# Where the row maxima of an attention step are kept: SBUF tile or spare columns of the PSUM tile

## The chip, the cores and the metric

The kernel runs on one core of one Trainium2 chip. The metric is the device time of one execution in microseconds, the median of several runs. A core has five engines that work through their own instruction queues and wait for each other by semaphores: TensorE (PE in the profile; PEld is its weight load), VectorE (DVE), ScalarE (ACT), GpSimd (POOL) and SyncE (SP, which here only issues transfers). TensorE writes its results to PSUM; VectorE and ScalarE reach both PSUM and the large on-chip memory SBUF; GpSimd works on SBUF alone in this kernel.

## The reference

Two layers in a row, for 8 batch entries of 576 tokens.

```
scores = 0.125 * q @ k^T                        # 8 x 8 heads, 576 x 576, head size 64
thresh = max(scores, last axis) - tau           # tau = 0.02
scores = where(scores >= thresh, scores, -1e9)
attn   = exp(scores - max(scores));  attn /= sum(attn) + 1e-9
x      = attn @ v                               # heads side by side: 576 x 512
h      = relu(x @ w_in);  u, v = halves of h    # 512 each
v_n    = (v - mean) / sqrt(var + 1e-6)          # over the 512 columns
v_s    = w_spatial @ v_n + b_spatial            # mixes the 576 tokens
out    = (u * v_s) @ w_out
```

The first four lines matter here. Per row of scores a maximum is needed before the exponentials, and only scores within tau of it count.

## The kernel before, in words

The attention is cut into 144 steps, 18 for each batch entry. A step `g` takes 128 query rows of a pair of heads and all 576 keys of both, and runs through these functions:

- `scores` and `scores_end` (L685, L696, both through `part`, L672): 16 matrix products on TensorE (L678) write the scores of both heads into one of two PSUM tiles, `s_ring[g % 2]`. Such a tile is `[128, 1536]` fp32 (L130)[...]. The scores of head 0 lie from column 96 to 671, those of head 1 from column 864 to 1439 (`at = (96, 864)`, L658). The columns from 672 to 863 hold nothing.
- `top` (L702, called by the token `M`): one VectorE reduction (L705) reads both heads' scores from PSUM and writes the two negated row maxima into a small SBUF tile `negm`, `[128, 2]` fp32, taken from the pool `small`.
- Then a step goes one of two ways, fixed by the lists `ON_ACT` (L84) and asked by `on_act(g)` (L660). 83 of the 144 steps are thresholded on ScalarE, 61 on VectorE.
  - On ScalarE: `shift` (L708, token `B`) is one VectorE `tensor_scalar` (L711) that turns `negm` into (scale times) minus maximum plus tau, in place in SBUF. `spread` (L714, tokens `E` and `F`, one for each head) has ScalarE compute Prelu of score plus that bias with a slope of 1e30 below zero (L719), so that all scores under the threshold become hugely negative. `exps` (L737, token `Z`) takes the exponential of it all (L739).
  - On VectorE: no shift. `spread` takes exp of score minus maximum (L722), and `mask` (L731, token `W`) zeroes on VectorE what lies under exp(-tau) (L734).

So for a step on ScalarE the order is: reduction L705, shift L711, two activations L719, one activation L739; the shift can be asked for at once behind the reduction or some instructions later. The two PSUM tiles alternate, so the matrix products of step `g + 2` must wait until the activations of step `g` have read its scores.

The probabilities are then transposed by transfers (or by TensorE for some), multiplied with v (`pv`, L376 and L381, divided on VectorE at L388 and L390), and the second layer's matrix products (L529, L576, L605, L634) with their evictions are woven in between the steps. GpSimd rearranges and converts loaded data (L192, L215, L341) and does the normalization of v (`moe_v`: L545, L557 to L561); all of this goes from SBUF to SBUF.

The order of all of it on each engine is written out by hand: the strings in `ORDER` (L16) list tokens such as `M5:0` or `B5:0`, and `run_token` (L884) issues them one after the other under a manual schedule (L940). Neither a planner nor priorities move them. The four strings serve batch entries 0, 1, 2 and all later ones, so that from the third entry on the iterations are nearly alike. Tokens for the way that a step does not take are skipped (L897).

Of the kernel before, what the change touches and what calls it, by code (L numbers as in the profile page):

```python
# [8 lines left out]
F32 = mybir.dt.float32  # L9
# [78 lines left out]
def kernel(  # L88
# [17 lines left out]
    nc = tc.nc  # L106
    B, H, S, D = q.shape
    assert (B, H, S, D) == (8, 8, 576, 64)
    scale = 0.125
# [3 lines left out]
    P = 128  # L113
# [4 lines left out]
    small = ctx.enter_context(tc.tile_pool(name="small", bufs=6))  # L118
# [11 lines left out]
    s_ring = [ps_s.tile([P, 1536], F32, name=f"s{i}") for i in range(2)]  # L130
# [50 lines left out]
    def view(t, off, dims):  # L181

        return bass.AP(t.tensor, t.offset + off, [t.ap[0]] + dims)
# [476 lines left out]
    def on_act(g):  # L660

        return g % 18 in ON_ACT[min(g // 18, len(ON_ACT) - 1)]
# [37 lines left out]
    negm = {}  # L700

    def top(g):  # L702

        nm = negm[g] = small.tile([P, 2], F32, name="negm")
        nc.vector.tensor_reduce(out=nm, in_=view(s_ring[g % 2], at[0], [[at[1] - at[0], 2], [1, S]]), axis=AX.X,  # L705
                                op=ALU.max, negate=True)

    def shift(g):  # L708

        nm = negm[g]  # L710
        nc.vector.tensor_scalar(out=nm, in0=nm, scalar1=scale if steps[g][1] == 4 else 1.0,  # L711
                                scalar2=float(tau), op0=ALU.mult, op1=ALU.add)

    def spread(g, h):  # L714
# [146 lines left out]
    steps = []  # L861
# [22 lines left out]
    def run_token(tok, it):  # L884
# [15 lines left out]
        m = 2 * b + a[0] if a else 0  # L900
        if kind in "SGYMEFBZW":
            {"S": scores, "G": turn_bank, "Y": scores_end, "M": top, "E": lambda g: spread(g, 0),
             "F": lambda g: spread(g, 1), "B": shift, "Z": exps, "W": mask}[kind](g)
        elif kind in ("QA", "QB", "qa", "qb"):
            task("q", i, kind[1] in "Bb")[1 + (kind[0] == "q")]()
# [135 lines left out]
```

## Time and profile before

Time: 450.61 us, median of 3 runs (450.59 to 450.75). Span of the profiled execution: 448.5 us; the granted clock of TensorE was 0.996.

| engine | busy us | share of the span | instructions |
|---|---|---|---|
| TensorE products | 416.1 | 93% | 5035 |
| VectorE | 400.8 | 89% | 615 |
| ScalarE | 388.6 | 87% | 649 |
| GpSimd | 176.9 | 39% | 403 |

| operation | count | busy us | mean ns |
|---|---|---|---|
| L705 reduction, VectorE | 144 | 194.5 | 1351 |
| L711 shift, VectorE | 83 | 22.0 | 265 |
| L719 Prelu, ScalarE | 166 | 115.3 | 744 |
| L739 exp, ScalarE | 67 into p, 16 into pr | 78.3 for the 67 | 1173 for the 67 |
| L734 mask, VectorE | 61 | 86.7 | 1422 |
| L192 copies into qn, GpSimd | 31 | 20.1 | 648 |

How to read it: all three big engines are busy around nine tenths of the time, and the loop over the batch has a period of 51.05 us in its later, like iterations. A busy time counts from an instruction's start to its end, and contains any time in which it was held up after its start. The profile's chain view follows the work that ended last back from the end, step by step to what released it; the waits view adds up by pair who waited for whom; the view of one line lists the shortest, the median and the longest duration of its instructions.

### The profile page before, as it was taken

Reading aid. Unit: us, or ns where it says so; the run is one execution under the profiler, and the core shown is the slowest. Engines: PE = TensorE matmul, PEld = TensorE weight load, DVE = VectorE, ACT = ScalarE, POOL = GpSimd, SP = SyncE. Lnnn points to the kernel's source line nnn. Section 1 sums busy time; section 2 is a strip of 40 time slices with the busy share of each in tenths; the row PEclk is TensorE's granted clock in tenths of the full one; section 3 lists DMA queues with packets and bytes.
Section 4 is the critical chain, followed back from the end, with each engine's and each line's share of the span. In section 5 each row is a group of like instructions: output and inputs, shape, how many; then the busy total and the mean of one; then the engine's idle time right before and its main releaser. Section 6 shows DMA issues by size and latency. Waiting matters only on the chain.

```text
span 448.5 us, 12858 instructions
## 1 busy us (share of the span) xinstructions
PE 416.1 (93%) x5035; PEld 260.2 (58%) x5035; DVE 400.8 (89%) x615; ACT 388.6 (87%) x649; POOL 176.9 (39%) x403
## 2 busy tenths in 40 slices
PE   6776879998999899999999999999999999999995
PEld 4455556565656665666565666566665666566542
DVE  5868889899999889999999999999989999999673
ACT  3897989998989899999899988999899998999351
POOL 1256333583225724354333533255333523344021
PEclk9989999999999999999999999999999999999999
DMA  7999899899999989999999999999899996896713
GB/s 206 277 245 204 230 235 184 140 206 211 214 153 235 229 175 209 198 226 237 189 193 209 248 186 184 233 217 239 187 199 213 265 179 107 161 198 122 176 36 107
DMA packets 222556, 88.15 MB, mean 197 GB/s; under 512 B 193568, under 2 KB 218272, under 8 KB 222496
## 3 DMA queue, kind: packets, MB, share of 16 engines
q1 hardware_dynamic: 221840, 86.45, 93.5%
q8 instruction: 40, 0.66, 0.6%
q0 software_dynamic: 160, 0.52, 0.3%
q10 hardware_dynamic: 496, 0.36, 0.2%
q14 instruction: 20, 0.16, 0.1%
HBM read 32.79 MB, written 9.44 MB: 94 GB/s over the span
## 4 chain that ended last, share of the span: by engine, by line
PE 48%; DVE 24%; ACT 18%; issue 6%; POOL 2%; DMA 1%; ACTq 0%; POOLq 0%; DVEq 0%
PE s L678 20%; DVE negm L705 13%; ACT e L722 6%; ACT e L719 5%; PE f L605 5%; PE f L329 4%; PE f L576 4%; DVE p L734 3%; PE f L529 3%; PE f L381 3%; DVE xn L390 2%; ACT p L739 2%; DVE negm L711 2%; PE f L514 1%; PE f L634 1%
## 5 line engine op out<-in xcount | busy, mean ns | idle before, releaser
L705 DVE TENSOR_REDUCE negm<-s 128x2 f32<-128x1152 f32 x144 | 194.5, 1351 | 19.8 <-PE s L678 16.4
L678 PE MATMUL s<-qkT 64*64 64x160 f32 (+1 forms) x2304 | 173.2, 416 | 12.3 <-ACT e L719 7.6
L678 PEld LDWEIGHTS s<-qkT 64*64 64x64 f32 x2304 | 107.4, 132 | 67.8 <-ACT e L719 17.1
L719 ACT ACTIVATE e<-s,negm 128x576 f32<-128x576 f32 x166 | 115.3, 744 | 19.0 <-DVE negm L711 11.3
L722 ACT ACTIVATE e<-s,negm 128x576 f32<-128x576 f32 x122 | 85.8, 756 | 7.4 <-DVE negm L705 7.1
L734 DVE SCALAR_TENSOR_TENSOR p<-e,ctau 128x1152 bf16<-128x1152 f32 x61 | 86.7, 1422 | 3.5 <-ACT e L722 3.2
L739 ACT ACTIVATE p<-e 128x1152 bf16<-128x1152 f32 x67 | 78.3, 1173 | 0.4
L215 POOL CAST v<-vl 128x512 bf16<-128x512 f32 x32 | 21.0, 658 | 79.0 <-PE s L678 72.8
L381 PE MATMUL f<-v,pT 128*128 128x65 bf16 x1008 | 44.6, 194 | 0.0
L381 PEld LDWEIGHTS <-pT 128*128 128x128 bf16 x1024 | 41.6, 98 | 2.4 <-issue 0.4
L545 POOL TENSOR_SCALAR nmean<-sm 128x1 f32<-128x1 f32 (+1 forms) x35 | 16.1, 468 | 55.5 <-PE s L678 34.5
L390 DVE TENSOR_TENSOR xn<-f,r 128x256 bf16<-128x256 f32 (+1 forms) x93 | 35.4, 380 | 2.9
L605 PE MATMUL f<-wsT,vn 128*128 128x512 bf16 x135 | 33.6, 380 | 0.0
L576 PE MATMUL f<-xT,w_in 128*128 128x512 bf16 x120 | 30.8, 380 | 0.6 <-DVE xn L390 0.3
L376 PE MATMUL f<-v,pT 128*128 128x130 bf16 x126 | 27.7, 220 | 2.1 <-DVE r L388 1.5
L192 POOL COPY qn<-ql 128x512 f32<-128x512 f32 x31 | 20.1, 648 | 21.3 <-PE s L678 20.5
L561 POOL TENSOR_SCALAR vn<-vrel,rs,nm 128x512 bf16<-128x512 f32 (+1 forms) x35 | 26.8, 767 | 3.8
L529 PE MATMUL f<-w_in,xT 128*128 128x512 bf16 x112 | 27.9, 379 | 0.2 <-ACT vrel L537 0.2
L551 ACT ACTIVATE sq<-vrel,nmean 128x512 bf16<-128x512 f32 (+1 forms) x35 | 25.8, 739 | 1.7 <-POOL nmean L545 1.6
L634 PE MATMUL f<-w_o,gT 128*128 128x512 bf16 x100 | 25.0, 380 | 1.4 <-ACT qkT L309 1.4
L341 POOL COPY qkT<-qkT 64x64 f32<-64x64 f32 x32 | 7.5, 235 | 40.7 <-PE s L678 21.0
L711 DVE TENSOR_SCALAR negm<-negm 128x2 f32<-128x2 f32 x83 | 22.0, 265 | 1.7
(158 smaller groups left out, 570.8 us busy)
## 6 DMA issues: line engine op xcount, KB each, us to landing
vl<-in_v_dram SPq DMA_DIRECT2D x16, 512.0 KB, 4.9
kl<-in_k_dram SPq DMA_DIRECT2D x15, 512.0 KB, 4.8
ql<-in_q_dram SPq DMA_DIRECT2D x15, 512.0 KB, 4.9
out_dram<-oo SPq DMA_DIRECT2D x12, 512.0 KB, 4.3
uT<-in_moe_w_in_dram SPq DMA_DIRECT2D x3, 512.0 KB, 4.9
uT<-in_moe_w_spatial_dram SPq DMA_DIRECT2D x2, 576.0 KB, 4.8
vx<-in_v_dram SPq DMA_DIRECT2D x16, 64.0 KB, 3.6
pT<-p SPq DMA_TRANSPOSE x64, 5.8
```

The costliest lines, as they stand in the source:

```text
L381: nc.tensor.matmul(out=t[:, at + 65 * h:at + 65 * h + 65], lhsT=pt[:, 5 * h + j, :], rhs=vt[:, 6 * h + j, :], start=False, stop=(h == 1 an ...
L390: nc.vector.tensor_tensor(out=dst, in0=o[ps, g0:g1, 0:64], in1=r[ps, g0:g1].unsqueeze(2).broadcast_to([ps.stop - ps.start, g1 - g0, 64]), ...
L529: nc.tensor.matmul(out=t, lhsT=x_of(b, f, slice(c * P, (c + 1) * P)), rhs=w_in[:, f, 512:1024], start=(f == 0), stop=(f == 3))
L576: nc.tensor.matmul(out=t, lhsT=w_in[:, m, f * P:(f + 1) * P], rhs=x_of(b, m, slice(0, 512)), start=(m == 0), stop=(m == 3))
L605: nc.tensor.matmul(out=t, lhsT=vn[:, c, f * P:(f + 1) * P], rhs=wsT[:, c, 0:512], start=(c == 0), stop=(c == 4))
L678: made.append(nc.tensor.matmul(out=s_ring[g % 2][halves[k], at[h] + lo:at[h] + hi], lhsT=qks[n][halves[h], 0, m:m + 64], rhs=qks[n][halves ...
L705: nc.vector.tensor_reduce(out=nm, in_=view(s_ring[g % 2], at[0], [[at[1] - at[0], 2], [1, S]]), axis=AX.X, op=ALU.max, negate=True)
L711: nc.vector.tensor_scalar(out=nm, in0=nm, scalar1=scale if steps[g][1] == 4 else 1.0, scalar2=float(tau), op0=ALU.mult, op1=ALU.add)
L719: nc.scalar.activation(out=e, in_=s, func=ACT.Prelu, bias=bias_, scale=scale if steps[g][1] == 4 else 1.0, alpha=1e30)
L722: nc.scalar.activation(out=e, in_=s, func=ACT.Exp, bias=bias_)
L734: nc.vector.scalar_tensor_tensor(out=numerators(g), in0=ef, scalar=ctau, in1=ef, op0=ALU.is_ge, op1=ALU.mult)
L739: nc.scalar.activation(out=numerators(g), in_=e_ring[g % 3].rearrange("p h s -> p (h s)"), func=ACT.Exp)
```

## The change

For the 83 steps that are thresholded on ScalarE, the reduction writes the two negated maxima to columns 704 and 705 of the step's own PSUM tile, which hold nothing else, instead of to an SBUF tile. The shift reads them there and writes its result to the SBUF tile `negm`, which is now taken from the pool at that point; the activations read their bias from it as before. So the shift goes from PSUM to SBUF where it went from SBUF to SBUF in place. The 61 steps that are masked on VectorE stay as they were. What it is for: the intermediate maxima are kept out of SBUF, so that the shift has one SBUF operand, its output, only.

```diff
     def top(g):
 
-        nm = negm[g] = small.tile([P, 2], F32, name="negm")
+        if on_act(g):
+            nm = s_ring[g % 2][:, 704:706]
+        else:
+            nm = negm[g] = small.tile([P, 2], F32, name="negm")
         nc.vector.tensor_reduce(out=nm, in_=view(s_ring[g % 2], at[0], [[at[1] - at[0], 2], [1, S]]), axis=AX.X,
                                 op=ALU.max, negate=True)
 
     def shift(g):
 
-        nm = negm[g]
-        nc.vector.tensor_scalar(out=nm, in0=nm, scalar1=scale if steps[g][1] == 4 else 1.0,
+        nm = negm[g] = small.tile([P, 2], F32, name="negm")
+        nc.vector.tensor_scalar(out=nm, in0=s_ring[g % 2][:, 704:706],
+                                scalar1=scale if steps[g][1] == 4 else 1.0,
                                 scalar2=float(tau), op0=ALU.mult, op1=ALU.add)
```

## The prediction

> **What bounds the kernel now.** I read, in this order, the busy shares and the chain that ended last, the groups around the two lines that the diff edits, the single instructions of those lines, the moments at which the slow ones happen, and the chain there.
>
> ```profile
> PE 416.1 (93%) x5035; PEld 260.2 (58%) x5035; DVE 400.8 (89%) x615; ACT 388.6 (87%) x649; POOL 176.9 (39%) x403
> ...
> PE 48%; DVE 24%; ACT 18%; issue 6%; POOL 2%; DMA 1%; ACTq 0%; POOLq 0%; DVEq 0%
> ...
> L705 DVE TENSOR_REDUCE negm<-s 128x2 f32<-128x1152 f32 x144 | 194.5, 1351 | 19.8 <-PE s L678 16.4
> ...
> L711 DVE TENSOR_SCALAR negm<-negm 128x2 f32<-128x2 f32 x83 | 22.0, 265 | 1.7
> ```
>
> No engine bounds alone: three are at 87 to 93% and the chain hops between them. What strikes is the last line. An operation on two elements takes 265 ns on average, as if it did real work. Its own view and those of its neighbours say why (min/median/max in ns):
>
> ```profile
> L711 DVE TENSOR_SCALAR negm<-negm x83: 149/169/871, 11.2 to 413.0; 128x2 f32<-128x2 f32 x83
> ```
> ```profile
> L705 DVE TENSOR_REDUCE negm<-s x144: 1340/1350/1359, 8.6 to 413.5; 128x2 f32<-128x1152 f32 x144
> ```
> ```profile
> L303 DVE TENSOR_SCALAR qkT<-f x12: 673/682/693, 34.9 to 398.5; 128x512 f32<-128x512 f32 x12
> ```
>
> The two VectorE operations that read PSUM (s and f are PSUM tiles) never vary by more than 20 ns. The one that goes SBUF to SBUF is 0.15 to 0.17 us mostly, but 26 of the 83 take over 0.2 us in the timeline, and the mean says that 83 x (0.265 - 0.16) = 8.7 us of its 22.0 us is stretch. The timeline at two of the long ones:
>
> ```profile
> 198.93 0.77 POOL L561 TENSOR_SCALAR vn<-vrel,rs,nm 128x512 bf16<-128x512 f32 x1
> 199.12 0.60 DVE L711 TENSOR_SCALAR negm<-negm 128x2 f32<-128x2 f32 x1
> ...
> 222.15 0.61 POOL L192 COPY kn<-kl 128x512 f32<-128x512 f32 x1
> 222.18 0.60 DVE L711 TENSOR_SCALAR negm<-negm 128x2 f32<-128x2 f32 x1
> ...
> 222.88 1.38 ACT L719 ACTIVATE e<-s,negm 128x576 f32<-128x576 f32 x2 [0.44 <-DVE negm L711]
> ```
>
> The GpSimd operations end at 199.70 and 222.76, the two L711 at 199.72 and 222.78: the small operation ends 20 ns after GpSimd lets go. ScalarE stands idle meanwhile (0.44 us in the last row). Over the run the waits table has this:
>
> ```profile
> ACT e L719 <- DVE negm L711: 11.3, 28, 1.2
> ```
>
> And the chain of the iteration from 184 to 236 us (an iteration of the batch loop repeats every 51.05 us) has both on it:
>
> ```profile
> 199.12 0.60 DVE negm L711
> ...
> 222.18 0.60 DVE negm L711
> ```
>
> [...] the PSUM readers L303 and L705 never stretch while GpSimd is busy 39% of the span. [...] a PSUM-to-SBUF copy of 512 columns takes 678 ns and of 128 columns 286, so (678 - 286)/384 = 1.02 ns a column and a fixed 155 ns, as much as a free L711. No row here shows VectorE writing PSUM.
>
> **The change part by part.** The instruction lists of both kernels, set side by side, hold the same instructions in the same order on every engine. A few matrix products also wait for VectorE now, but for something that the ScalarE operation they already wait for came after; and a handful of reductions wait for an earlier VectorE one, long done[...]. Those I cost at nothing. The move of the tile's allocation into the shift is naming only.
>
> (a) The 83 shifts read PSUM. The fixed 155 ns of the copies plus two columns gives 0.16 us, free of GpSimd: 83 x 0.16 = 13.2 us instead of 22.0, so 8.7 us less VectorE time. Bounds on one: 0.15 us (the fastest L711)[...].
>
> (b) The 83 reductions write two columns to PSUM. Nearest row: themselves, 1.35 us[...]. I take 20 ns. It shows only where someone waits for the write: 50 of the 83 shifts follow their reduction directly. That is 50 x 0.02 = 1 us[...], a share of it on the chain.
>
> (c) How much of (a) lies on the path. Listing L711 in the chain over the whole run gives, above a free 0.15: 0.45 at eight places (199, 222, 250, 273, 301, 324, 352 and 375 us), and 0.72 (18.9), 0.37 (94.0), 0.13 (98.8), 0.44 (110.1), 0.39 (171.2), 0.34 (403.4): 3.6 + 2.4 = 6.0 us. The other 2.5 us are beside other work.
>
> (d) How much of the 6.0 survives, since the next-longest path is close. At 199: VectorE then runs without a pause until the reduction at 203.42, whose scores TensorE gives at 201.90 + 1.20 = 203.10, so at most 0.3 us is won. It reaches TensorE: the eight products L576 from 204.27 last until 206.34, 2.07 us, though four take 0.86 on the chain, so 0.35 us in it is waiting for VectorE's xn. At 222: ScalarE idles 0.44 us for it and then runs on nearly without a pause to 231; TensorE's pause before the products L634 at 228.39, behind ScalarE's qkT, is 228.39 - (226.91 + 1.13) = 0.35 us, from the start of its scores and their 1.13 us. So 0.3 + 0.35 = 0.65 of the 0.9 us survives. Both shifts follow their reduction directly: minus 2 x 0.02, 0.6 us an iteration. Four like iterations: 2.4 us. The 2.4 us of the others by the same share, 0.65/0.9: 1.7 us. A further 0.1 to 0.3 us goes to (b) at free shifts on the chain. Sum 3.8 us: 450.6 - 3.8 = 446.8.
>
> **The rivals.** First, absorbed: TensorE is busy 50.2 of the 51.05 us of an iteration, so a tie behind VectorE might leave only 0.1 us an iteration; 450.6 - 0.8 = 449.8. For it: TensorE's share. Against: busy there contains waiting, as the 2.07 us show. Second, slower: [...] Against: reads from PSUM show no extra here. Third, larger: delays off the chain count too, because they hold back the evictions and so TensorE's slots; all 8.7 us come back: 442. Against: only 28 waits of ScalarE name L711, and 2.5 us of the stretch are in the shadow of ScalarE work.
>
> **How the numbers follow.** Forecast (445 to 449) 0.70; absorbed 0.12; slower 0.09; larger 0.09. The point is the forecast's. The range leaves out slower, most of larger and the upper part of absorbed: 444.1 to 450.2. Its lower end is the whole 6.0 us of the chain with a little more. Faster by over 0.2% means under 449.7: 0.70 + 0.09 + nearly half of absorbed = 0.84; same 0.07; slower 0.09.
>
> **What would show it.** In the changed kernel the shift should read 0.15 to 0.18 us in minimum, median and maximum, about 13 us in all; the reductions that write s 1.34 to 1.42 us; VectorE busy about 392 us; ScalarE's wait for the shift down from 11.3 to about 7 us; the period of an iteration about 50.45 us. If the shift is flat but the period stays at 51, the ties were nearer than I read them (absorbed). [...] A chance new meeting of VectorE's two-input mask with GpSimd, from shifted times, could spoil some of it too.

## The result and the profile after

The changed kernel takes 446.59 us (446.43 to 446.77, 4 runs) against 450.68 us before: ratio 0.9907, 95% interval 0.989 to 0.9924. That is 4.1 us less, where 3.8 us were forecast (446.8).

The engines' busy times, from the page of the changed kernel:

```profile
PE 413.9 (93%) x5035; PEld 260.5 (59%) x5035; DVE 394.1 (89%) x615; ACT 388.5 (87%) x649; POOL 181.9 (41%) x403
```

VectorE's time fell by 6.7 us and TensorE's by 2.2; GpSimd's rose by 5.0, so it is not GpSimd that is relieved. (The rise lies in the 64 small casts of L221: their median is 236 ns where it was 235, but the longest takes 1464 ns where it took 239; why is not known.) The shift, now L714, and the reduction, now L708 (min/median/max in ns), each from the view of its line:

```profile
L714 DVE TENSOR_SCALAR negm<-s x83: 146/159/163, 12.0 to 409.2; 128x2 f32<-128x2 f32 x83
```
```profile
L708 DVE TENSOR_REDUCE s<-s x83: 1350/1366/1367, 10.6 to 407.8; 128x2 f32<-128x1152 f32 x83
L708 DVE TENSOR_REDUCE negm<-s x61: 1340/1350/1359, 9.3 to 409.8; 128x2 f32<-128x1152 f32 x61
```

The shift has become as steady as the other readers of PSUM: 146 to 163 ns, a range of 17, as L303 had one of 20 in the kernel before; there the shift went up to 871. Laying the start and end of each shift beside those of the GpSimd instructions shows what it no longer waits for. In the kernel before, 41 of the 83 shifts begin while a GpSimd instruction runs, and none ends before that instruction does; all 26 that take over 200 ns end 21 to 27 ns after the end of a GpSimd instruction. In the changed kernel 43 begin so, and 26 of them end before it. The shift's group, with busy us and mean ns behind the bar, fell from 22.0 to 12.9 us:

```profile
L714 DVE TENSOR_SCALAR negm<-s 128x2 f32<-128x2 f32 x83 | 12.9, 155 | 1.7
```

The 83 reductions that write PSUM take 16 ns more at the median than the 61 in the same kernel that write SBUF. The waits table shows who profits:

```profile
ACT e L723 <- DVE negm L714: 6.3, 18, 0.6
```

ScalarE waited for the shift 28 times, 11.3 us, and now 18 times, 6.3 us. The place that stood at 222 us before, from the timeline of the changed kernel:

```profile
220.06 1.20 PE L678 MATMUL s<-qkT 64*64 64x160 f32 x16
...
220.45 0.61 POOL L192 COPY kn<-kl 128x512 f32<-128x512 f32 x1
220.48 0.16 DVE L714 TENSOR_SCALAR negm<-s 128x2 f32<-128x2 f32 x1
220.67 0.69 DVE L619 TENSOR_TENSOR gT<-f,uT 128x512 bf16<-128x512 f32 x1
220.73 1.38 ACT L723 ACTIVATE e<-s,negm 128x576 f32<-128x576 f32 x2
...
221.45 1.37 DVE L708 TENSOR_REDUCE s<-s 128x2 f32<-128x1152 f32 x1
```

GpSimd's copy starts at 220.45 and runs until 221.06; the shift starts 30 ns into it, as before, and now ends at 220.64 without minding it. ScalarE follows at 220.73 with no wait.

The period of the batch loop is read from the same reduction one batch entry apart. In the chain of the kernel before:

```profile
220.79 1.37 DVE negm L705
...
271.83 1.37 DVE negm L705
```

and in that of the changed kernel:

```profile
320.19 1.38 DVE s L708
...
370.56 1.38 DVE s L708
```

51.04 us before, 50.37 us after: 0.67 us an entry. (In one entry of the changed kernel, at 252 us, VectorE pauses 0.30 us for nothing that the profile names; that entry takes 50.74 us.) Laying the start times of all 144 reductions of both traces side by side gives the rest: the changed kernel's profile starts 0.75 us behind, is 0.6 us ahead at the end of the first entry, and 3.7 us ahead at the end. The 0.75 us belong to the first loads and not to the change: in the twelve experiments the first reduction starts anywhere from 8.5 to 9.7 us.

### The profile page after: what moved, and what is told of

Same layout as the page of the kernel before. It is cut to its first block, busy times and chain, and to the rows that moved or that the text cites. A ratio compares the mean times of both kernels' runs of the same rounds, so it can differ in the third digit from the quotient of the medians.

```text
span 444.7 us, 12872 instructions
## 1 busy us (share of the span) xinstructions
PE 413.9 (93%) x5035; PEld 260.5 (59%) x5035; DVE 394.1 (89%) x615; ACT 388.5 (87%) x649; POOL 181.9 (41%) x403
## 4 chain that ended last, share of the span: by engine, by line
PE 34%; DVE 25%; ACT 16%; issue 7%; DMA 3%; POOL 2%; DVEq 0%; POOLq 0%; ACTq 0%
PE s L678 14%; DVE p L738 7%; DVE s L708 6%; ACT e L726 6%; DVE negm L708 5%; PE f L605 5%; ACT e L723 5%; PE f L576 3%; PE f L329 3%; PE f L381 2%; DVE xn L390 2%; ACT p L743 2%; ACT sq L551 1%; PE f L529 1%; DMA pT<-p 1%
## 5 line engine op out<-in xcount | busy, mean ns | idle before, releaser
L708 DVE TENSOR_REDUCE s<-s 128x2 f32<-128x1152 f32 x83 | 113.1, 1363 | 12.8 <-PE s L678 10.4
L708 DVE TENSOR_REDUCE negm<-s 128x2 f32<-128x1152 f32 x61 | 82.5, 1352 | 8.6 <-PE s L678 6.6
L738 DVE SCALAR_TENSOR_TENSOR p<-e,ctau 128x1152 bf16<-128x1152 f32 x61 | 86.4, 1417 | 3.3 <-ACT e L726 3.2
```

What stands on the lines that cost most here:

```text
L738: nc.vector.scalar_tensor_tensor(out=numerators(g), in0=ef, scalar=ctau, in1=ef, op0=ALU.is_ge, op1=ALU.mult)
```

## The experiments

Two theories stood against each other. The first goes by the name of port theory in what was expected: the shift was held because it went from SBUF to SBUF, as a `tensor_scalar`, while GpSimd was at work; the 26 slow ones end 21 to 27 ns behind a GpSimd instruction. It is no more than a name: what in the chip holds the shift was not shown. The other side has three forms: it was slow because it overwrote what had just been written, or because the maxima lay in SBUF at all, or the gain comes from order and allocation and is spread over all shifts. All ratios are against the kernel before, run on the same chip.

**Two SBUF tiles, not in place.**

```diff
-        nm = negm[g] = small.tile([P, 2], F32, name="negm")
+        nm = negm[g] = small.tile([P, 2], F32, name="rawm" if on_act(g) else "negm")
 ...
-        nm = negm[g]
-        nc.vector.tensor_scalar(out=nm, in0=nm, ...
+        raw = negm[g]
+        nm = negm[g] = small.tile([P, 2], F32, name="negm")
+        nc.vector.tensor_scalar(out=nm, in0=raw, ...
```

> The shift is no longer in place: the reduction writes one SBUF tile and the shift reads it and writes another SBUF tile. Port theory (the shift goes from SBUF to SBUF and so waits for GpSimd): nothing changes, the shift still takes 149 to about 870 ns, some 22 us in all, the period stays at 51.05 us, the time at 450.7. In-place rival (the shift was slow because it overwrote the tile that the reduction had just written): the shift drops to some 0.16 us each and the time to about 446.6.

Measured: 450.69 us, ratio 1.0001 (0.9991 to 1.0011). The view of the shift:

```profile
L712 DVE TENSOR_SCALAR negm<-rawm x83: 153/169/875, 12.0 to 413.2; 128x2 f32<-128x2 f32 x83
```

These are the figures of the kernel before to within 4 ns at the minimum and the maximum, with the same median. The in-place rival falls, and with it the later allocation of the tile, which this kernel has too.

**Maxima in SBUF, tau in PSUM.** The maxima stay where they were; the shift gets a second tensor operand that lies in PSUM.

```diff
-        nc.vector.tensor_scalar(out=nm, in0=nm, scalar1=scale if steps[g][1] == 4 else 1.0,
-                                scalar2=float(tau), op0=ALU.mult, op1=ALU.add)
+        nc.vector.scalar_tensor_tensor(out=nm, in0=nm, scalar=scale if steps[g][1] == 4 else 1.0,
+                                       in1=s_ring[g % 2][:, 706:708], op0=ALU.mult, op1=ALU.add)
 ...
+        for t in s_ring:
+            nc.vector.memset(t[:, 706:708], float(tau))
```

> The maxima stay in the SBUF tile, in place, but the shift is a scalar_tensor_tensor whose second tensor is tau, laid once into spare columns of the PSUM tiles: one SBUF input, one PSUM input. Port theory: [...] it never stretches (about 0.15 to 0.18 us), the reductions stay at 1350 ns, and the time is that of the changed kernel or up to 0.5 us less, 446.1 to 446.7. Staging rival (it is keeping the maxima in PSUM that helps, whatever the form of the shift): the shift stretches as before, 450.7.

Measured: 446.05 us, ratio 0.9891 (0.9876 to 0.9906).

```profile
L711 DVE SCALAR_TENSOR_TENSOR negm<-negm,s x83: 145/156/159, 11.8 to 409.2; 128x2 f32<-128x2 f32 x83
```

In place, SBUF in, SBUF out, and it never stretches. So it is not where the maxima are kept that matters, but that the instruction is no longer a `tensor_scalar` with both sides in SBUF. The staging rival falls. The time lies just below the 446.1 us that were expected at the least. One might ask whether the other form of the instruction is enough, without PSUM. A shift of that form with both tensors in SBUF was not run, but the mask (L734 before) is one on more columns, and it can be held: it took 2119 ns at most, and 1417 at the median, under the added GpSimd work below.

**The 26 slow steps alone, and the 57 others alone.** `in_psum(g)` selects the steps that are changed; the rest is as before. The lines are given against the changed kernel, and the shift chooses its source in the same way.

```diff
-        if on_act(g):
+        if on_act(g) and in_psum(g):
             nm = s_ring[g % 2][:, 704:706]
 ...
```

> Only the 26 steps whose shift took over 0.2 us in the kernel before keep their maxima in PSUM; the other 57 stay in SBUF. Port theory: all or nearly all of the gain, 446.3 to 447.3 (a few of the 57 may newly meet GpSimd as times move). Rival that the gain is spread over all shifts or comes from their order or allocation: 26/83 of 4.1 us, about 449.4.

> The other way round: the 57 steps whose shift was short before keep their maxima in PSUM, the 26 slow ones stay in SBUF. Port theory: no gain, and a price of 57 x 16 ns for the reduction's write to PSUM where it shows, 450.6 to 451.5; the 26 shifts stay at 0.2 to 0.9 us. Rival that the gain is spread over all shifts: 57/83 of 4.1 us, about 447.9.

Measured: the 26 alone 446.18 us, ratio 0.9902 (0.9887 to 0.9917); the 57 alone 450.46 us, 0.9993 (0.9985 to 1.0002). Both lie 0.1 us below the ranges expected for the port theory, and far from the rival's 449.4 and 447.9. The shifts of the first kernel, and of the second:

```profile
L722 DVE TENSOR_SCALAR negm<-negm x57: 152/169/259, 12.1 to 409.9; 128x2 f32<-128x2 f32 x57
L722 DVE TENSOR_SCALAR negm<-s x26: 149/159/163, 19.7 to 405.9; 128x2 f32<-128x2 f32 x26
```
```profile
L722 DVE TENSOR_SCALAR negm<-s x57: 145/155/161, 12.1 to 413.4; 128x2 f32<-128x2 f32 x57
L722 DVE TENSOR_SCALAR negm<-negm x26: 169/443/606, 20.6 to 409.4; 128x2 f32<-128x2 f32 x26
```

The whole gain lies in the 26, nothing in the 57, and 57 writes to PSUM cost nothing that can be measured.

**More GpSimd work in both kernels.** One copy from SBUF to SBUF that nobody needs, in each step:

```diff
+    spare = const.tile([P, 3, P], BF16, name="spare")
 ...
         follow(turned[g], opened[g])
+        nc.gpsimd.tensor_copy(out=spare, in_=view(identf, 0, [[0, 3], [1, P]]))
```

> The kernel before with one more GpSimd copy of 128 x 384 elements, SBUF to SBUF, that nobody needs, in each of the 144 steps. Port theory: the shift meets GpSimd more often, its mean goes from 265 ns to 320 ns or more and its sum from 22 to over 26 us, and the kernel is slower than the one with the same copies and the maxima in PSUM by more than the 4.1 us of now. Rival that GpSimd has nothing to do with it: the shift stays at 265 ns, and the difference between the two kernels at about 4 us.

> The changed kernel with the same 144 superfluous GpSimd copies. Port theory: the shift stays at 146 to 165 ns; what the copies cost here (a later GpSimd queue, the two-input mask of VectorE[...] meeting them) is not the shift's, a time of 447 to 453 us, and below the kernel before with the copies by over 4.1 us. Rival: the shift varies here too.

Measured: before with the copies 459.05 us (ratio 1.0181, 1.0154 to 1.0207), changed with the copies 453.93 us (1.0061, 1.0046 to 1.0077): 5.1 us apart instead of 4.1. The runs of these two kernels scatter too much for that difference to count (the second one's from 450.53 to 455.36), but the period in the later entries is steady: 51.77 against 50.61 us, 1.16 apart where it was 0.67. GpSimd's busy time went to some 271 us in both. The shift before, and after:

```profile
L714 DVE TENSOR_SCALAR negm<-negm 128x2 f32<-128x2 f32 x83 | 26.5, 319 | 1.7
```
```profile
L717 DVE TENSOR_SCALAR negm<-s 128x2 f32<-128x2 f32 x83 | 12.8, 155 | 1.7
```

More GpSimd work lengthens the shift that goes SBUF to SBUF, 265 to 319 ns, and leaves the one that reads PSUM at 155. The dose has its effect, though the mean fell just short of the 320 that was named. In the first kernel 46 of the 54 shifts that begin while a GpSimd instruction is on record end after it, the other 8 before; those began 2 to 118 ns behind its start, and which of the two really came first is not shown, since spans on GpSimd are rough.

The copies cost the changed kernel over 7 us as well, more than the 453 us expected at most, and this is not the shift's. Of the 7.0 us by which its last reduction is late, 5.9 have arisen before the fourth batch entry begins (161.1 and 167.0 us); by what there was not followed up. One part can be read from the mask, which took 1554 ns at most in the changed kernel. With the copies:

```profile
L741 DVE SCALAR_TENSOR_TENSOR p<-e,ctau x61: 1402/1417/2119, 12.0 to 420.4; 128x1152 bf16<-128x1152 f32 x61
```

The nine longest of them, 1507 ns and over, end 1201 to 1220 ns after the end of a GpSimd instruction that ran around their start. In the kernel before, the six longest, 1465 to 1595 ns, end 1202 to 1227 ns after one likewise. So this `scalar_tensor_tensor`, whose two tensors both lie in SBUF, is held beside GpSimd as well, for up to 0.7 us over its median here; the form alone does not protect it. The masks' sum went from 86.4 to 88.9 us.

**Where in an iteration the gain arises.** The same edit, with `in_psum(g)` true for one or two steps of the batch entries 3 to 7 only.

> Maxima in PSUM only for step 3 of the batch entries 3 to 7 (the shift that stood at 222.18 us, 0.60 us long, in the kernel before); all else as before. The prediction's reckoning of this place (ScalarE idles 0.44 us for the shift, TensorE pauses 0.35 us): 0.35 us an iteration, period 50.70 us. The reading of the changed kernel's profile (the next reduction is then held by its scores, which TensorE delivers at 221.66 + 1.31 us whatever VectorE does): about 0.13 us, period 50.9 us.

> Maxima in PSUM only for step 13 of the batch entries 3 to 7 (the shift at 199.12 us, 0.60 us long). The prediction's reckoning (the reduction at 203.42 cannot start before its scores at 203.10): 0.3 us an iteration, period 50.75 us. If the ties are nearer: under 0.15 us, period over 50.9 us.

> Maxima in PSUM only for step 10 of the batch entries 3 to 7 (the shift that stood at 190.33 us, 0.42 us long, in the kernel before, not on the chain that ended last, with five instructions between it and its reduction's successor). The prediction counts it at nothing: period 51.05 us. The reading of the changed kernel's trace, where the reduction after it comes 0.24 us sooner and 0.11 us of that is lost by the next but one: 0.1 to 0.25 us, period 50.80 to 50.95 us.

> Maxima in PSUM only for the steps 10 and 13 of the batch entries 3 to 7. If the two add up, as the reductions' start times in the changed kernel say (0.13 and 0.42 us): period about 50.5 us, which with step 3's 0.11 us makes up nearly all of the 0.68 us of the whole change. If step 10 gives nothing in company either: 50.76 us, as with step 13 alone.

| steps changed | period us | saved an entry | time us | ratio, 95% interval |
|---|---|---|---|---|
| none (before) | 51.04 | | 450.68 | |
| 3 (shift at 222 us) | 50.93 | 0.11 | 450.47 | 0.9992, 0.9985 to 0.9999 |
| 13 (at 199 us) | 50.76 | 0.28 | 449.59 | 0.9968, 0.9958 to 0.9979 |
| 10 (at 190 us) | 50.82 to 50.95 | 0.09 to 0.22 | 449.60 | 0.9978, 0.9969 to 0.9988 |
| 10 and 13 | 50.53 | 0.51 | 448.27 | 0.9952, 0.9936 to 0.9968 |
| all | 50.37 | 0.67 | 446.59 | 0.9907, 0.989 to 0.9924 |

The times of the kernel before on the chips of these runs are 450.76 us (steps 3 and 13) and 450.63 us (10, and 10 and 13). The periods are differences of the start of the same reduction in the like entries, four in each trace. One or two of the four are longer by some 0.2 to 0.4 us, from a single pause (51.27 before, 50.76 twice with steps 10 and 13), and the table has the others. Whole runs agree with it: divided by the five entries changed, the ratios give 0.07 us an entry for step 3, 0.29 for step 13, 0.20 for step 10 and 0.43 for the pair. The pair saves 0.51 by the period; with step 3, 0.62 of 0.67. Step 10 gives about 0.2, though its shift is not on the chain that ended last.

**Is tau in PSUM the better version?** Both on one chip.

> The shift with the maxima in SBUF and tau in PSUM, beside the changed kernel on the same chip, to see which is the better. Same mechanism, and the reduction writes SBUF, 1354 against 1363 ns: 83 x 9 ns = 0.75 us of VectorE time, of which a fifth to a half shows, so 0.1 to 0.4 us below the changed kernel. If the reduction's write is hidden altogether: the same time.

> The changed kernel itself, for that comparison: 446.6 us, 0.1 to 0.4 us above the one with tau in PSUM if the write to PSUM shows.

Measured: tau in PSUM 445.82 us, 0.9891 (0.9874 to 0.9907); the changed kernel 446.60 us, 0.9907 (0.9893 to 0.9922). Twice the median lies 0.5 to 0.8 us lower, in this pair by more than the 0.1 to 0.4 expected of the reduction's write, but the intervals overlap and the periods in the last entries are the same (50.35 and 50.37 us). That it is better is not shown; that it is as good is.

## Why the prediction was right

**The cause**, that the shift is held inside its own bar while GpSimd works and is free of it when it reads PSUM, was right and is now shown by more than a coincidence of end times: the shift's stretch stays when it is merely taken out of place, goes when one operand comes from PSUM, and grows with GpSimd's work in the one kernel alone. Taken out of place it took 875 ns at most, with its second tensor in PSUM 159, read from PSUM 163. The runs show the hold and what takes it away; by what means a GpSimd instruction holds the shift, none of them shows.

**(a) The shift's cost**: 0.16 us each and 13.2 us in all were forecast; 155 ns and 12.9 us measured. The longest shift of the changed kernel took 163 ns.

**(b) The reduction's write**: 20 ns taken, an assumption with no row of the kernel before behind it, 16 measured at the median, and no cost in time with 57 of them alone.

**VectorE's busy time** fell to 394.1 us and not to the 392 forecast, which took off the shift's fall alone. Two things were left out. The reductions' own rise, which (b) had put at 83 x 20 ns, is 1.1 us (194.5 before, 113.1 and 82.5 after). And this line counts stretches in which two instructions overlap once: the starts and durations of all VectorE instructions have the shifts overlap their neighbours by 8.9 us before and 7.7 after, so that of the 9.1 us by which their durations fell 1.2 were no gain for the line.

**(c) and (d), the part that survives**: 0.6 us an iteration and 50.45 us were forecast; 0.67 and 50.37 measured. The sum was right, its split was not.

**Step 13**, at 199 us: 0.3 forecast from the scores that arrive at 203.10, 0.28 measured alone. The term stands.

**Step 3**, at 222 us: 0.35 forecast, 0.11 measured alone. The step that failed is the sentence that ScalarE's idle 0.44 us and TensorE's pause of 0.35 us would both close. They rest on the shifts behind this one, and those on a reduction whose scores I had checked at 199 and not here. In the kernel before:

```profile
221.77 1.20 PE L678 MATMUL s<-qkT 64*64 64x160 f32 x16
...
223.29 1.34 DVE L705 TENSOR_REDUCE negm<-s 128x2 f32<-128x1152 f32 x1
...
228.39 1.89 PE L634 MATMUL f<-w_o,gT 128*128 128x512 bf16 x8 [0.27 <-ACT qkT L309]
```

The scores stood at 221.77 + 1.20 = 222.97 and the reduction began at 223.29, 0.32 us later. In the changed kernel, by the lines shown further up, they stood at 220.06 + 1.20 = 221.26 and the reduction began at 221.45, 0.19 us later, although VectorE's instruction before it had ended at 221.36. So only some 0.13 us were there to be won. Further on in the changed kernel:

```profile
223.58 1.37 ACT L723 ACTIVATE e<-s,negm 128x576 f32<-128x576 f32 x2 [0.42 <-DVE r L388]
...
225.11 1.20 PE L678 MATMUL s<-qkT 64*64 64x160 f32 x16
...
226.55 1.89 PE L634 MATMUL f<-w_o,gT 128*128 128x512 bf16 x8 [0.23 <-ACT qkT L309]
```

ScalarE did start its activations at 220.73, 2.15 us before the 222.88 of the kernel before, where all around it led by 1.71; but it then stood idle for 0.42 us until the next step's pair at 223.58, which led by 1.84 us only. TensorE's pause, reckoned as in the prediction, is 226.55 - (225.11 + 1.13) = 0.31 us: it did not close, it shrank by 0.04.

**Step 10**, at 190 us: nothing forecast, since (c) counted only shifts on the chain, and about 0.2 us measured. TensorE's scores and its transposes behind them (L329), before and after:

```profile
190.14 1.20 PE L678 MATMUL s<-qkT 64*64 64x160 f32 x16
...
191.43 0.63 PE L329 MATMUL f<-identf,kn 128*128 128x128 f32 x4
```
```profile
188.97 1.20 PE L678 MATMUL s<-qkT 64*64 64x160 f32 x16
...
190.11 0.66 PE L329 MATMUL f<-identf,kn 128*128 128x128 f32 x4
```

The transposes began 1.29 us after the scores before, 1.14 us in the changed kernel. The chain shows that pause of 0.15 us only as a slightly longer run of TensorE. By the code these transposes write one of two PSUM tiles f, which VectorE's divisions behind the shift empty; that this is the link was argued from the code and not tried.

So two errors, 0.24 too much and 0.2 too little an entry, cancelled; that the total came within 0.3 us of the measured gain is in part luck. Of the shifts outside the like iterations, 1.7 us were forecast; laid side by side, the reductions show some 1.2 us won around the one at 18.9 us alone, where the share of 0.65/0.9 gave 0.5, and little at 94.0, 171.2 and 403.4 us. Around the one at 110.1 us some 0.4 us are won, where the share gave 0.3. Applying one share to all was good for the sum and for few of its terms. (The 2.5 us that (c) has beside other work should read 8.7 - 6.0 = 2.7; no term of the sum rests on it.)

**The rivals.** Absorbed: TensorE's busy 50.2 of 51.05 us an iteration did contain waiting, and its busy time fell with the change, 416.1 to 413.9 us. Slower: that PSUM costs more was an assumption that no trace had shown; a shift that reads it takes 159 ns at the median where it took 169, and a reduction that writes it 16 ns more than one that writes SBUF. Larger, 442 us: the off-chain shift of step 10 did count, as that rival had it, but only by 0.2 us an entry.

## What to carry to other kernels

When the longest duration of a tiny instruction is several times its shortest, as with 871 and 149 ns here, suspect that it waits inside its own bar, and look for an engine whose instruction ends just before it does. Here it was enough to change the form of the small one: it helped to have its one source in PSUM (163 ns at most), and it helped as much to give it a second source there (159). A chain view gives the place of a gain but neither its size nor all of its places: at each place, ask of every input of the next instruction when it would arrive if the delay were gone, and look for pauses that the chain shows only as a slightly long run. To find where a small gain arises, change single steps and read the period of a regular loop, which here told 0.1 us apart where single runs scatter by more.

## What the runs showed of the hardware

- In the kernel before, 26 of 83 `tensor_scalar` on 2 columns from SBUF to SBUF took over 200 ns and ended 21 to 27 ns after a GpSimd instruction, in one case over two in a row: that one took 871 ns, the shortest of the group 149. The same work read from PSUM, or as `scalar_tensor_tensor` with one tensor in PSUM, took 145 to 163 ns in all 83 cases, and 26 of these, read from PSUM, ended while a GpSimd instruction that they began beside still ran.
- Such a shift was no slower with its two columns read from PSUM (changed kernel) than from SBUF (before): medians 159 and 169 ns, shortest 146 and 149.
- In the changed kernel a VectorE reduction of 1152 columns that writes its two results to PSUM took 1366 ns at the median, one that writes them to SBUF 1350.
- A `scalar_tensor_tensor` on 1152 columns with both tensors in SBUF took 1410 ns at the median and 1595 at most in the kernel before, 1417 and 2119 in the changed kernel with the added GpSimd copies.
